# Three more of 28 key sums formed on GpSimd, and a newly computed order of all instructions

## The chip, the cores and the metric

One core of a Trainium2 chip runs the whole program. Its engines work side by side and meet at semaphores: PE (TensorE, matrix products), PEld (its weight loads), DVE (VectorE), ACT (ScalarE), POOL (GpSimd) and SP, which only issues DMAs. The metric is the device time of one execution in microseconds. The kernel before took 998.01 us (median of three runs, 996.77 to 999.7).

## The reference

For 8 batches, 8 heads, 576 positions and head size 64, the kernel computes linear attention with random features and feeds its output to a gated network:

```
phi(x)  = exp(x omega^T - |x|^2/2 - max) / sqrt(128)       x = q or k, scaled by 64^(-1/4)
num     = phi(q) (phi(k)^T v),   den = phi(q) sum_s phi(k) + 1e-6
x       = num / den, as rows of 512                        4608 tokens
out     = silu(x w_in) w_out                               512 -> 2048 -> 512
```

The sum over positions of phi(k), one vector of 128 features for each head, is what this document calls the key sum.

## The kernel before, in words

**Attention.** Heads are taken in pairs: 32 pairs n = 0 to 31, four to a batch. For a pair, PE projects keys and queries (`project` L554, and the shared middle block L560) into PSUM; DVE takes maxima (L569, L567) and shifts (L575); ACT (L592), for some pairs DVE (L600, L597) and then ACT, makes the exponentials `hk` and `hq`. PE forms phi(k)^T v (L713), and the key sum. DVE multiplies `hq` with the key sum and adds up (L701, `denom`), and takes the reciprocal `rd` (L706). POOL scales `hq` by it (L731), PE transposes it (L737) and forms the numerator (L773). Pairs 0 to 3 get their key sum as a column of another product (L651); the other 28 in one of two ways:

```
def zsum_direct(n, ps):          # pairs 4 to DIRECT - 1: PE alone, fp32
    for j in range(2):
        nc.tensor.matmul(..., sides_of[:, j], e[:, MID], ...)          # L641
        for i in range(4):
            nc.tensor.matmul(..., ones, e[:, 5 * j + i], ...)          # L643
def zsum(n, ps):                 # pairs DIRECT to 31: after POOL's five sums and a split
    for i in range(2):
        nc.tensor.matmul(ps[:, : 2 * M], ones_r, zp[:, i], ...)        # L635, fp32r
```

In the second way POOL first adds the blocks of `hk` into `t` (two of L615, one L617, two L621), rounds that to fp32r (`zp`, L626) and takes the rest (L630). PE then needs two fp32r products over 256 columns in place of ten fp32 products over 128.

**The network.** Every fp32 product of the network is made of three fp32r products (high by high, high by low, low by high). The first three batches go through both layers in the usual way: 16 steps f of 128 hidden units each, L948 for the first layer, L1194 for the second. The rest goes through a seven-product block scheme (L1033 first layer, L1147 second). The weights come in as 64-bit numbers: SP loads them, ACT and DVE rebuild fp32 words (L871, L873, L877 on DVE), POOL rounds to fp32r (L890) and takes the rest (L894). The 16 expansion weights w0 to w15 are needed by L948 at step f = 0 to 15 of the first batch, so all of this falls into the first 180 us, beside the attention of the early pairs.

**The order.** Nothing is scheduled on the chip: each engine runs its queue in the order in which the program was written. A planner in the kernel (`Plan.run`) makes that order before the build. It walks through all units of work with a table of costs (`COST` and `Plan.cost`), waits that it thinks worth taking (`WAIT_PE` and the like) and a key for each unit; the keys are moved by a long table of numbers (`SHIFTS`). The mark DIRECT also decides that for pairs after it the middle projection of the next pair shares a PSUM bank with a transpose (`mid_turn`), and that the small transpose of phi(k)^T v (L721) is issued inside a transpose unit; both issue the same matmuls.

Of the kernel before, what the change touches and what calls it, by code (L numbers as in the profile page):

```python
# [36 lines left out]
DIRECT = 8  # L37
# [18 lines left out]
for _f in range(16):  # L56
# [37 lines left out]
EASE = 0.075  # L94
# [11 lines left out]
    "nb": (0.29, 0.37), "vo": (0.3, 0.4), "dv": (1.25, 1.35), "tt": (0.54, 0.72), "ssum": (0.66, 0.745), "den": (3.41, 3.49),  # L106
# [10 lines left out]
    "AIBFNlBoBOAIAIAIAIApBkCNAIAIAIAIAIAIAIFBAIE3BkBpAIDrXvX-AIgAN4AIIrAIHRAISPAIA4AIAI-4AIAI+1m0E1AQY+BlAIAIV2GuVU"  # L117
    "SBLvMTDIWaBdE4g0N6BTSRSySyICKqsIR1gAAIEsNFA9fLBbECHyAIAIOAAIAUDL3PB5KVQqAmYoNLIWKmJSFLR6CSSkCNQnRQkVmxAIAIMQGa"
    "IfNyCEB5FigAQjAIsXAIowAI0OAIk7AIDxatOoF1gMqeAQCzXoVkB5AIAIFADkF5DzMcNKLNLLXVXXAIAIOwC2BmA3AIAIFvgANfFxj-AYSuAy"
    "McFlDlAIAIAIBAAIAIqUuwAIDsAIAIKxNGRn-4Q2r5S4MrmOiZ9nQbQSAIAINyCxBzAIPSDxCNenNIQVDD4DAIFPAQE2AI2BTGMtCy-4AIrhAI"  # L120
    "EcbS2qy0rA4lxxV7AIAIAIAIB9AIG3AIAwDECfMcs7Bgucbo-41sWs-4e793rN+ThC9aaOAfvmAIUH2y55sUlN740mPt-1h7821N-43g72-4l0"
    "E2o0zDr6kXx-YJ6s2X5WlO9I-4AIFDv7B2AI6Lu5I0UecHAIpivfe4bjX2TvOnTydYdOatC5E3LHLjxRMABFaSbJTaw289ejIQjbk+iselsruu"
    "tDyttvecpw-47QE2rZV4MadOm9Wwmfe8+t-WUGmK3abhpwFofCuzpdUDAIgIR4hCsbAiV3A6kV1tiDSjjzZavXGEBTH+AxCYKNAIAIis28YRmD"
    "EdkkOLdtqq4EAIAyA+p7lYAIHQDU0LgfrqAyYE1+9L-21oAIypYkcxoqYoZQ-WTKbdS+eg1Ci1Zd1q+wj5AIPai5RTGLbSsE1NJepCSpOA0jlx"
    "NB2GEiGdgCX3otpcn+otWkjcoVe5iXbUo1mhBf78wOVzlO7lrmqmmnfiBk3+avT+FCXRz3-j0MlfdiRab0iMN3i0baW6l7g4rd7iHfmhvjzkHD"
    "AJTjgZKdcGvcPLdHlYKefKdCT1nFM5k2RNblYanVw1GneWAIecUwt4fMhuZpR9Iwa5Ij69ZLfJvcAIEpF+BQQlAJjmCTRZcPCmNTHthxfUZ-AI"
    "BRXmYLQAIZR3ldNQq4S9FaOTCkOsMghgdKWyAIAIWAAIBcEUGeDOAIBSEZCMAIJhNWhaoGXG0lAIdJAIAIBjAIAIAIAIAIRpAIBQZtzlAgoFAI"
    "AIOoKSgpJONZHIAIprCgHvp7kijCrAjzn6AwAOAIBpAwPYnPCpLdMEqGXPAICPsvw4W09aOPLxRxBfIAAIKIARH+B8AIFHKfeUdnGXIvAIAIPg"
# [64 lines left out]
)  # L193
HOT = 100.0
PULSE = 0.24
IDLE = 1.237
PAD = 1.63
EARLY = 0.9

# [80 lines left out]
class Plan:  # L280
# [20 lines left out]
    def cost(self, u):  # L301
# [1507 lines left out]
```

## Time and profile before

| | |
|---|---|
| median of three runs | 998.01 us |
| the profiled execution | 997.93 us, of which 996.1 us span from the first instruction to the last |
| PE busy | 978.1 us (98%) |
| DVE / ACT / POOL busy | 744.2 / 634.7 / 380.6 us |
| granted TensorE clock | 0.995 of full speed on average |
| PE share of the chain that ended last | 80%, DVE 10% |

The span is what the trace covers; 1.8 us lie around it. Busy time is a union of instructions, so PE at 98% means that it had nothing in flight for 18 us. In a timeline a matmul's duration is its latency; how long it holds PE is read from one start to the next. An fp32 product shows as two records, an fp32r product as one.

### The profile page before, as it was taken

The numbers are of one execution on the slowest core, as the hardware profiler recorded it, in microseconds if no ns is written. First come the engines' busy times: TensorE is split into PE (matmuls) and PEld (weight loads), VectorE is DVE, ScalarE is ACT, GpSimd is POOL, SyncE is SP. The second block draws the span as 40 slices with busy tenths as digits, with TensorE's granted clock in tenths as the row PEclk, the third lists the DMA queues.
The fourth block names the chain that finished last, engine by engine and source line by source line (L and its number), as shares of the span: only waits on it lengthen the run. The fifth ranks groups of instructions, "written<-read, shape, count | busy, mean of one in ns | idle before, by whom it ended". The sixth has DMA issues, their size and how long they took to land.

```text
span 996.1 us, 17264 instructions
## 1 busy us (share of the span) xinstructions
PE 978.1 (98%) x5748; PEld 786.4 (79%) x5748; DVE 744.2 (75%) x1851; ACT 634.7 (64%) x1231; POOL 380.6 (38%) x483
## 2 busy tenths in 40 slices
PE   8999999999999999999999989999999999999998
PEld 7878877778787877777778778878888877888886
DVE  6999889676877557898676999895359977556853
ACT  6988677356666667867788666579676444334541
POOL 0255654777878786556672033223021000000000
PEclk8999999999999999999999999999999999999999
DMA  9787777687776877678887667866545787555582
GB/s 347 263 268 253 272 233 258 198 283 245 232 244 221 292 251 222 193 229 306 295 275 252 206 222 239 261 215 195 190 151 170 231 275 230 190 193 189 187 290 86
DMA packets 107592, 232.94 MB, mean 234 GB/s; under 512 B 14704, under 2 KB 39408, under 8 KB 107504
## 3 DMA queue, kind: packets, MB, share of 16 engines
q1 hardware_dynamic: 107344, 231.58, 70.6%
q8 instruction: 46, 0.75, 0.3%
q14 instruction: 42, 0.34, 0.1%
q10 hardware_dynamic: 160, 0.26, 0.1%
HBM read 182.52 MB, written 49.28 MB: 233 GB/s over the span
## 4 chain that ended last, share of the span: by engine, by line
PE 80%; DVE 10%; ACT 4%; POOL 3%; DMA 2%; issue 2%; SPq 0%; POOLq 0%; DVEq 0%; ACTq 0%
PE ps_acc L1033 19%; PE ps_acc L1147 15%; PE ps_acc L1194 11%; PE ps_h L948 7%; PE ps_fx L948 4%; PE ps_att L554 3%; PE ps_att L1147 3%; PE ps_att L1033 2%; PE ps_att L713 2%; PE ps_h L1147 2%; DVE prod L701 1%; PE ps_att L773 1%; PE ps_att L737 1%; PE ps_h L1033 1%; PE ps_fx L1147 1%
## 5 line engine op out<-in xcount | busy, mean ns | idle before, releaser
L1033 PE MATMUL ps_acc<-w,x 128*128 128x512 f32 x816 | 197.8, 396 | 0.0
L1033 PEld LDWEIGHTS ps_acc<-w,x 128*128 128x128 f32 x816 | 150.5, 188 | 33.9 <-DVE w L1080 0.3
L731 POOL TENSOR_TENSOR hq<-hq,rd 128x384 f32<-128x384 f32 x84 | 75.4, 922 | 167.1 <-DVE rd L706 166.9
L1194 PE MATMUL ps_acc<-wo,gh 128*128 128x512 f32 x384 | 123.1, 401 | 0.0
L1147 PE MATMUL ps_acc<-w,x 128*128 128x512 f32 x426 | 107.7, 395 | 0.2 <-DVE w L1137 0.2
L948 PE MATMUL ps_h<-x,w 128*128 128x512 f32 x384 | 102.7, 402 | 1.6 <-POOL w L894 0.6
L1147 PEld LDWEIGHTS ps_acc<-w,x 128*128 128x128 f32 x426 | 79.4, 188 | 18.8 <-DVE w L1137 0.9
L948 PEld LDWEIGHTS ps_h<-x,w 128*128 128x128 f32 x384 | 68.8, 188 | 18.2 <-POOL w L894 1.1
L1194 PEld LDWEIGHTS ps_acc<-wo,gh 128*128 128x128 f32 x384 | 68.6, 188 | 14.2
L1194 PE MATMUL ps_acc<-wo,gl 128*128 128x512 f32 x192 | 75.4, 393 | 0.0
L1147 PE MATMUL ps_acc<-gh,x 128*128 128x512 f32 x196 | 69.6, 396 | 0.0
L701 DVE CUSTOM_DVE_ANT_0 prod<-hq,ps_att 128x128 f32<-128x128 f32 (+1 forms) x170 | 48.8, 287 | 14.4 <-PE ps_att L635 8.6
L615 POOL TENSOR_TENSOR t<-hk 128x256 f32<-128x256 f32 x48 | 38.8, 823 | 47.3 <-ACT hk L606 30.1
L1091 DVE TENSOR_TENSOR gl<-gf,gh 128x512 fp32r<-128x512 f32 x48 | 42.5, 888 | 16.0 <-ACT gf L1087 16.0
L948 PE MATMUL ps_fx<-x,w 128*128 128x512 f32 x192 | 49.4, 398 | 0.0
L1147 PEld LDWEIGHTS ps_acc<-gh,x 128*128 128x128 f32 x196 | 36.8, 188 | 8.6
L537 ACT ACTIVATE nat<-nat 128x576 f32<-128x576 f32 x58 | 39.9, 695 | 4.8 <-DMA nat<-kn 3.4
L1194 PEld LDWEIGHTS ps_acc<-wo,gl 128*128 128x128 f32 x192 | 36.0, 188 | 8.4 <-DVE gl L1091 0.4
L948 PEld LDWEIGHTS ps_fx<-x,w 128*128 128x128 f32 x192 | 35.2, 188 | 7.8 <-issue 0.2
L747 ACT COPY en<-ps_att 128x384 f32<-128x384 f32 x56 | 27.0, 491 | 18.6 <-PE ps_att L737 13.2
L1147 PE MATMUL ps_acc<-gl,x 128*128 128x512 f32 x98 | 38.3, 391 | 0.0
L569 DVE TENSOR_REDUCE smq<-ps_att 128x4 f32<-128x512 f32 x44 | 29.0, 683 | 9.9 <-PE ps_att L554 9.4
(475 smaller groups left out, 2408.2 us busy)
## 6 DMA issues: line engine op xcount, KB each, us to landing
x<-ws SPq DMA_DIRECT2D x84, 512.0 KB, 3.6
x<-wt SPq DMA_DIRECT2D x44, 512.0 KB, 3.7
wo<-wo_d SPq DMA_DIRECT2D x32, 512.0 KB, 4.4
x<-wo_d SPq DMA_DIRECT2D x64, 256.0 KB, 3.2
rawq<-qT SPq DMA_DIRECT2D x30, 352.0 KB, 5.0
rawk<-kT SPq DMA_DIRECT2D x30, 352.0 KB, 4.3
v<-v SPq DMA_DIRECT2D x28, 320.0 KB, 4.0
nat<-kn SPq DMA_DIRECT2D x29, 288.0 KB, 4.3
```

The source lines that it names most:

```text
L537: nc.scalar.activation(nat, nat, AF.Square, scale=SCALE * 0.5**0.5)
L554: nc.tensor.matmul(ps[:, i * M : (i + 1) * M], raw[r, o : o + P], oms[r], start=True, stop=True)
L569: nc.vector.tensor_reduce(m[:, 5 * j : 5 * j + 4], ps.rearrange("p (c m) -> p c m", m=M), AX.X, ALU.max)
L615: nc.gpsimd.tensor_tensor(t[:, step], e[:, 5 * step : 5 * step + 2], e[:, 5 * step + 2 : 5 * step + 4], ALU.add)
L701: nc.vector.tensor_tensor_reduce(out=prod[r], in0=e[r, c], in1=z[r, j * M : (j + 1) * M], scale=1.0, scalar=GUARD, op0=ALU.mult, op1=ALU.a ...
L731: nc.gpsimd.tensor_tensor(e[:, c], e[:, c], rd[:, c].unsqueeze(2).broadcast_to([P, 3, M]), ALU.mult)
L747: nc.scalar.copy(T["en", n][:, 3 * g * P : 3 * (g + 1) * P], T.pop(("t", n, g)))
L948: nc.tensor.matmul(ph, w[:, i], x[:, j], start=k == 0 and n == 0, stop=k == NK - 1 and n == 2)
L1033: nc.tensor.matmul(ph, ws[:, u, kk * P : (kk + 1) * P], o[:, x], start=i in (0, 1, 4) and kk == 0 and n == 0, stop=kk == 1 and n == 2, ski ...
L1091: nc.vector.tensor_tensor(gl, T.pop(("gf", t, f)), T["gh", t, f].bitcast(F32), ALU.subtract)
L1147: nc.tensor.matmul(T["qb", p, chain][d], w[:, u, d * P : (d + 1) * P], x, start=i in (0, 1, 4) and s == 0 and n == 0, stop=s == NS - 1 and ...
L1194: nc.tensor.matmul(T["po", t][j], g[:, js], w, start=f == 0 and n == 0, stop=f == NF - 1 and n == 2)
```

## The change

DIRECT falls from 8 to 5, so that pairs 5, 6 and 7 (the sixth to the eighth) get their key sums through POOL and fp32r as pairs 8 to 31 did. Some costs of the planner and its waits are set anew, and the table of keys is a new one, so that the order of every engine changes.

```diff
-DIRECT = 8
+DIRECT = 5
-STAY = 9.083
+STAY = 20.466
-CALM = 0.133
-JOIN = 7.97
-WAIT_PE = 0.223
-WAIT_ACT = 0.222
-WAIT_DVE = 0.181
-WAIT_POOL = 0.175
-HASTE = 2.024
+CALM = 0.163
+JOIN = -0.122
+WAIT_PE = 0.281
+WAIT_ACT = 0.128
+WAIT_DVE = 0.175
+WAIT_POOL = 0.019
+HASTE = 8.0
-    "nb": ..., "vo": (0.3, 0.4), "dv": (1.25, 1.35), ...
+    "nb": ..., "vo": (0.555, 0.575), "dv": (1.375, 1.46), ...
 SHIFTS = (
-    "AIBFNlBoBOAIAIAIAIApBkCNAIAIAIAIAIAIAIFBAIE3BkBpAIDrXvX-AIgAN4AIIrAIHRAISPAIA4AIAI-4AIAI+1m0E1AQY+BlAIAIV2GuVU"
...
+    "AIAINlAIA4AIG7AIAIAIAKATGfAIALARAIAIHbGMFBAIE3BkBpAIDrFzI1IPgADuAIDoAIUiAIkqAIR1AIAI-4DCAIAIH1AIAIAIEVAIAIlvL3T7"
...
-IDLE = 1.237
-PAD = 1.63
+IDLE = 3.287
+PAD = 2.265
```

Over the whole program PE issues 24 fewer of L643, 6 fewer of L641 and 3 fewer of the filler products L506 (which stood in a wait near the start), and 6 more of L635. POOL issues 21 more instructions: 6 of L615, 3 of L617, 6 of L621, 3 of L626 and 3 of L630. DVE, ACT and SP have as many instructions of each kind as before. The PE queue changes between fp32 and fp32r products 248 times after its first L948, in place of 252.

**PE at the key sum of the sixth pair.** Before, it stands in the middle of the second layer's products of an early step (`sides` and `ones` are constants, `hk` the exponentials):

```order
L1194 MATMUL ps_acc<-wo,gl 128x512
L641 MATMUL ps_att<-hk,sides 128x128
L643 MATMUL ps_att<-hk,ones 128x128 x4
L641 MATMUL ps_att<-hk,sides 128x128
L643 MATMUL ps_att<-hk,ones 128x128 x4
L560 MATMUL ps_fx<-oms,rawk 128x128
L1194 MATMUL ps_acc<-wo,gh 128x512 x2
```

Now, in PE's queue (`zp` is what POOL made of `hk`, `w_1091` the expansion weight w3):

```order
L721 MATMUL ps_acc<-ident,kt 128x128
L560 MATMUL ps_acc<-oms,rawq 128x128
L635 MATMUL ps_fx<-zp,ones_r 128x256 x2
L554 MATMUL ps_att<-oms,rawk 128x128 x8
L948 MATMUL ps_fx<-x_415,w_1091 128x512 x3
```

The ten fp32 products became two fp32r products, and they stand earlier: before the first product with w3, where they stood behind w4's.

**POOL at the same place.** Before, its queue goes from the scaling of the fifth pair (L731) straight to the weights w3 (`w_1050`) and w4 (`w_1121`):

```order
L894 TENSOR_TENSOR wo<-w_812,wo 128x512
L731 TENSOR_TENSOR hq<-hq,rd 128x384 x3
L890 CAST w_1050<-w_1025 128x512
L894 TENSOR_TENSOR w_1050<-w_1025,w_1050 128x512
L890 CAST w_1121<-w_1090 128x512
L894 TENSOR_TENSOR w_1121<-w_1090,w_1121 128x512
```

Now the sixth pair's sums stand in between (w3 is `w_1091`, w4 `w_1117`):

```order
L731 TENSOR_TENSOR hq<-hq,rd 128x384 x3
L615 TENSOR_TENSOR t<-hk 128x256 x2
L617 TENSOR_TENSOR t<-t 128x2x128
L621 TENSOR_TENSOR t<-t,hk 64x128 x2
L890 CAST w_1091<-w_1055 128x512
L626 CAST zp<-t 128x256
L890 CAST w_1117<-w_1079 128x512
L894 TENSOR_TENSOR w_1117<-w_1079,w_1117 128x512
L630 TENSOR_TENSOR zp<-t,zp 128x256
L894 TENSOR_TENSOR w_1091<-w_1055,w_1091 128x512
```

All seven sums of the pair stand ahead of the rest of w3; its rounding went in between.

**DVE at the words of w13.** Before, the last of the three word instructions (L877 on `w_2030`) ends a short run, and the reduction of the eighth pair (L701) comes behind it:

```order
L546 TENSOR_REDUCE smq<-nat 128x9
L600 TENSOR_TENSOR hq<-ps_att,nbq 128x512
L600 TENSOR_TENSOR hq<-ps_fx,nbq 128x512
L1091 TENSOR_TENSOR gl<-gf,gh 128x512
L871 TENSOR_SCALAR w_2030<-wraw 128x512
L873 SCALAR_TENSOR_TENSOR w_2030<-wre,w_2030 128x512
L877 SCALAR_TENSOR_TENSOR w_2030<-wraw,w_2030 128x512
L701 ISA prod,den<-hq,ps_att 128x128
```

Now (the words of w13 are `w_2088`; the run begins with the end of the eighth pair's reduction):

```order
L706 RECIPROCAL rd<-den 128x9
L569 TENSOR_REDUCE smq<-ps_att 128x4
L575 TENSOR_REDUCE smq<-smq 128x2x4
L575 TENSOR_REDUCE nbq<-smq 128x2x4
L877 SCALAR_TENSOR_TENSOR w_1939<-wraw,w_1939 128x512
L871 TENSOR_SCALAR w_2033<-wraw 128x512
...
L1091 TENSOR_TENSOR gl<-gf,gh 128x512 x2
L871 TENSOR_SCALAR w_2088<-wraw 128x512
...
L873 SCALAR_TENSOR_TENSOR w_2088<-wre,w_2088 128x512
L597 TENSOR_SCALAR hk<-ps_att,nbk 128x128
L877 SCALAR_TENSOR_TENSOR w_2088<-wraw,w_2088 128x512
```

Ahead of w13's last word instruction DVE now has one whole reduction more (ten L701, ten reads, one L706), four more of L569, four more of L600, one more of L1091, six more of L575 and one more each of L567 and L597, and of no kind fewer. On PE, ahead of the first L948 with w13, there are 24 more of L554, nine more of L737 and one more of L560, and the three direct sums (30 products) are replaced by six of L635.

## Rows read from the trace of the kernel before

**Rows 1.** First part of the page: busy time, share, instructions.
```profile
PE 978.1 (98%) x5748; PEld 786.4 (79%) x5748; DVE 744.2 (75%) x1851; ACT 634.7 (64%) x1231; POOL 380.6 (38%) x483
```

**Rows 2.** Windows: stretch, length, busy of PE, PEld, DVE, ACT, POOL; clock; DMA.
```profile
8.00:14.00 6.00, 5.84 (x40) 5.35 (x40) 5.48 (x13) 3.09 (x9) 0.00 (x0) 0.50 1.04 415
...
0.00:60.00 60.00, 53.48 (x475) 48.19 (x476) 48.49 (x140) 47.74 (x145) 13.01 (x21) 0.94 0.83 297
60.00:171.00 111.00, 110.38 (x673) 88.28 (x673) 99.40 (x237) 82.96 (x156) 61.40 (x59) 1.00 0.76 261
```

**Rows 3.** Timeline of PE, direct sums of the sixth and eighth pair: start, duration.
```profile
87.74 0.38 PE L641 MATMUL ps_att<-hk,sides 128*128 128x128 f32 x2
...
89.97 0.39 PE L560 MATMUL ps_fx<-oms,rawk 128*128 128x128 f32 x2
...
150.49 0.48 PE L641 MATMUL ps_att<-hk,sides 128*128 128x128 f32 x2
...
152.74 0.71 PE L1194 MATMUL ps_acc<-wo,gh 128*128 128x512 f32 x2
```

**Rows 4.** Timeline of PE at the ninth pair's sum, the first in fp32r.
```profile
196.08 0.40 PE L635 MATMUL ps_att<-zp,ones_r 128*128 128x256 f32 x2
196.32 0.63 PE L1194 MATMUL ps_acc<-wo,gh 128*128 128x512 f32 x2
```

**Rows 5.** Groups of POOL by line, all 24 key sums: busy us, mean ns; idle before.
```profile
L615 POOL TENSOR_TENSOR t<-hk 128x256 f32<-128x256 f32 x48 | 38.8, 823 | 47.3 <-ACT hk L606 30.1 <-ACT hk L592 17.1
L621 POOL TENSOR_TENSOR t<-t,hk 64x128 f32<-64x128 f32 x48 | 24.2, 504 | 21.8 <-ACT hk L592 18.9
L617 POOL TENSOR_TENSOR t<-t 128x256 f32<-128x256 f32 x24 | 19.0, 790 | 1.8
L630 POOL TENSOR_TENSOR zp<-t,zp 128x256 fp32r<-128x256 f32 x24 | 18.8, 783 | 1.8
L626 POOL CAST zp<-t 128x256 fp32r<-128x256 f32 x24 | 11.5, 481 | 1.4
```

**Rows 6.** Timeline of POOL at the weight w13.
```profile
153.38 0.61 POOL L890 CAST w<-w 128x512 fp32r<-128x512 f32 x1 [4.45 <-DVE w L877]
154.07 1.30 POOL L894 TENSOR_TENSOR w<-w,w 128x512 fp32r<-128x512 f32 x1
```

**Rows 7.** Timeline of PE at the first products with w13 and inside w15's.
```profile
156.51 2.91 PE L948 MATMUL ps_fx<-x,w 128*128 128x512 f32 x12
...
172.79 2.56 PE L948 MATMUL ps_h<-x,w 128*128 128x512 f32 x10 [0.63 <-POOL w L894]
```

**Rows 8.** Timeline of DVE: shifts, a split and one whole reduction.
```profile
150.18 0.68 DVE L600 TENSOR_TENSOR hq<-ps_fx,nbq 128x512 f32<-128x512 f32 x1
150.78 0.68 DVE L1091 TENSOR_TENSOR gl<-gf,gh 128x512 fp32r<-128x512 f32 x1
...
153.23 0.28 DVE L701 CUSTOM_DVE_ANT_0 prod<-hq,ps_att 128x128 f32<-128x128 f32 x1
...
156.51 0.22 DVE L706 RECIPROCAL rd<-den 128x9 f32<-128x9 f32 x1
```

**Rows 9.** DVE's L873: group from 60 to 171 us; durations min/median/max, whole run.
```profile
L873 DVE SCALAR_TENSOR_TENSOR w<-wre,w 128x512 uint32<-128x512 uint32 x24 | 20.0, 835 | 1.0 <-ACT wre L857 0.3
...
L873 DVE SCALAR_TENSOR_TENSOR w<-wre,w x32: 675/692/1595, 23.5 to 176.0; 128x512 uint32<-128x512 uint32 x32
```

**Rows 10.** Timeline of PE: the longest idle times in the middle; one at L635.
```profile
354.26 0.38 PE L635 MATMUL ps_fx<-zp,ones_r 128*128 128x256 f32 x1 [0.42 <-POOL zp L626]
...
581.50 1.31 PE L713 MATMUL ps_fx<-hk,v 128*64 128x128 f32 x20 [1.52 <-ACT hq L592]
584.63 0.49 PE L554 MATMUL ps_h<-oms,rawk 64*128 64x128 f32 x2 [0.84 <-ACT hq L592]
```

**Rows 11.** Timeline of PE near the start: projections behind a wait, the filler products.
```profile
8.16 2.08 PE L554 MATMUL ps_acc<-oms,rawk 64*128 64x128 f32 x16 [2.02 <-DMA rawk<-kT]
...
10.75 1.49 PE L506 MATMUL ps_acc<-ones 128*128 128x128 f32 x6
```

More of the change, by code (lines that the diff above doesn't have):

```diff
@@ L93 @@
 COLD = 8.5
-EASE = 0.075
+EASE = 0.086
 FORMS = {"s1": 0, "s2": 0, "m": 0, "m2": 0, "proj": 2, "kv": 3, "num": 3, "kvnum": 3}
@@ new lines @@
+    "orwx2PkVrJAIMOWenkVZwSQS6A5GwpXg5Q6Fah7lhkDajs1bl7FnNzlmFhQcrbsgrceUsGfilwZacfEPDfGpHUqjUXAIoVPIo0AILWdEdgMFtE"
+    "r1GuDSaBWbgOcoNbJYf3KZBcK+pojewOLEQ+VmC9E31PAI9sAqAIZ0AIml838H-4gqU+QpueyZJ0AITARTKxAU3ESxvHF5FFQoxrXvVlKhECCi"
+    "AICUAILgFdJVARAIDZGOqhDKAuDKEgcpZF-g+7YXPLE1-jW1AIFVD6vTvHAIulggsB-4y6IDxJxyZJ4dAIle-QE1Jzjjexj1xpqBK8KzTJCZDl"
+    "E+CVwLBcF5VvExNfCJBSbnCiJ5JlG6IpKeBcRvDkJ8BcBcBcBBJWZFXwJCDBh9EjFjAKCAr6joBCYtKEJUHyATRWFcWG7u3DCwj8-4-4u05tXj"
+    "5m4j279Prnvs44RExe-1yEuufE0mA8hBz887irzb9OLHxLG0hSxanCxrwp0BQR3x1adluIOwWGumhN-Xu1FFk1Knp5n84kfhWWrHH7H9AjXtAI"
@@ new lines @@
+    "ApFBCucpEgEgEtLBVWIgHMCcAI38d7AgcySeLCLqBFEgSAfKWwNNk1TOT5hmJgUvJtFUpQEyOLBhAIBYDoAQBlUiUv22qeKkh-FboEAIBklYhI"
+    "AaBGAIAIAIC9DXxEgKXpjgNXCLQiHtlfPCTWANAIudBIHXdVV5DkagIvNSGjW5S7I+bADoZPAIAIGoV2CFFsNIxwZwlv4AXCY7ohHCfQhZj9NQ"
+    "NEAkEXGGOemqW9ntT+O7Bvo9dH-4UFF9KnDgGfA4Q2MFtRASLtHCM3eCByLwIYNlAdL2AIAIc1AIFtBRD+D0nrX7PzFnYkXdYoyReRU-GUAIAN"
+    "AIYDYKITnRvGWSAIAh4Ra03MezK5gFhBZVB+o0STVIcfexV5n5BTJ3C4JFQPQ9gaUwAIVvRYF9AIKHw9uKD0A-Z3LNGUHrLJFR-4EzGLDPDPNF"
+    "CCondFEUAzDPD9qB-cUmCADxQqHuHCCftFFBcKe-bxvyFMeHECdtAIHFEmCQEZ6EQ3upBtL5AIBLAIwRTgkI-4eMhpOJcy6kCJ5FAIAIlVTXrA"
@@ new lines @@
+    "gliahpAVDC+jtX7+GQezZNWq+7PrtXSUoFngozrwr+Ifl8xFL+b9AIlogsBtjXmOwjhh-K9e6psoj7H7UANbAIvBt4iaktTRIxXYAIQhxwa0ro"
+    "x9juAIpQfvz8Jyq1JWUQfqWUh8PNtpy8dVUHeGYMwY7a5zm2aIcDB30m3mshi1AId4bPe+a7iNOjR-fJgNhXbfpXGpFgD-2LFGK4pOhLL8OBA3"
+    "B7vMiO2EQ1vNAIcwOhzm7SMYCz8gls8Y3wBouegQ2yAIxUAI45A0g9JvBulgAIv3rxeTlu4XnVgaAIbyVqF2pNIUyOtk2XxveoTH5fMzG7AIJd"
+    "bF5UBGw-AvE90WS9re5d9W0D5K4l6J+pFVvLsOTBD6jklw4AFflGHTCfC64xQnERGEEtF-AIfYF7AIF8DhKQDrE7F7F4NRMCNBLsAIXEoMIbIV"
+    "EcLuMcXpJhEtSAMbFZGHFyGYsmKBEtDxAlGzHRAIOHA5AIPYAIAICZAIDSYviQyK5W20MDKl4FgBCvDTDygPozK-AI-ESy-4FrCxEMAbAcCaBM"
@@ new lines @@
+    "IuBxBRXRpaJRVBCFByB8jFATAbAIAqAICmLnJINaF9AI95GAAf3-AMFcw4ZrYsmABOGRJIHFJjzLDMPaBKBFM3JfMrstTXoQAIAIFEDcZfBHCG"
+    "AdFSTje2TvMlayMAaWWITwAiAIJMGTNVJDHWP4AIIJlDDtBMq44WVDi2DTRp55iIETE34W-hOpAI1aExXVd-ZDbR9LMbAIAU+v+v84HIHTjlJN"
+    "aovu+UVTxqBVAIDwu5+vDM+UiyJKtZ+MSCUfE22ADrAIg6bxsb6BC4xuAIMyPQ0-0i21rnNlZ0FTRI2XTtrVvbD7AIWSfTng-4SUGnSzHUQ5lR"
+    "ZWh0YdkdnlPFOaN+KMF1MIfylbOvjxGuFa82B7AItFCbEYyu+Jk6-46vFFD-kepOxPCvAIa-aV-izFw1jqzdAIAI-Dm+zVcDbJJ4d1Amtzs5pR"
+    "h3w9AIAI6Xpx3yu9o7AITGC2HPkVcqMiP7NA5rs-J4IPBfOOEykUIzMSJjq6juhiSdYkBqJTNCmwIQqEAIDMS6Z8GOYGGlAsCTBulscgrFcmQl"
@@ new lines @@
+    "F13Jf8bzJ+SoJUs6SisaTsLFU1UgAIGGQPhkBYCHhauxVIAIHV-b-4nxRDCIckO1BrTDVoTYeVAIB1uO44dPHMCIuEtrAIqVCDAITiAIAIAIAr"
+    "AIPZCW-23QPlQNXANly0QZBDBqSyENJzsivc+bzcpaDK5czPnxDRAIcRHEZuUg118247CWAPdJwej7DXJsJBGXET7p0qoUfhIHtggecwZO3MCE"
+    "T4FdJtNWBWjnwNGhe7KPEUGa-teiKjDQEFOZILiQnNbuCAmuILF+JfAIElZDQDAITJRdep74VvYraQx1FMHjev7lTnS+XMb9ZCQrFXvMPVJ4sX"
+    "GiAOK+bo3FFvAIFvPmvKu47ThCwZH5C6-e4i0uv59t7nTstq+TAI2hPdtXCOcsttmk0owLjTlIok+3nGz8+pjl59tiiFQKWoIunj4OVUwdVUlk"
+    "uCIaAIEqlmHL1ACCK5j6lBWxrBvA65t9bND2XsakxpNPPCK4Ggs+Bnr6siadQjjrwnVxCf7shEciX6904FxelcVviwGsXUMMCkD7QeCkVvOyCk"
@@ L193 @@
+    "oPs2mDeNprl1l2rImepGmlrRnOi-h0pdrkoMlD"
 )
@@ L319, in cost @@
         if n[0] in ("kv", "num") and n[1] < SHARE:
-            return 2.25, 2.42
+            return (2.26, 2.47) if kind == "kv" else (2.18, 2.35)
         if kind == "kw" and n[1] < SHARE:
-            return 0.24, 0.35
+            return 0.15, 0.28
         if kind == "wd" and n[-1] == 0:
```

127 lines of the change are left out of this document (51 added, 76 removed).

## The prediction

> **What bounds the kernel now.** The page's first part comes first: PE has work in flight for 978.1 of 996.1 us, DVE for 744.2 and POOL for 380.6 [rows 1]. So PE is the bound, and there are only 18 us of idle PE time to win or to add to; whatever shortens PE's own work shortens the run, as long as PE does not wait instead. The windows come second, since a mean of 98% can hide a stretch with another limit. From 60 to 171 us PE has 110.4 of 111.0 us, but DVE has 99.4 too, and POOL 61.4 [rows 2]. In this stretch two engines are nearly full at once: DVE idles for 11.6 us there, and for 11.5 us before 60 us. Third, the timeline at the hand-over between them. The weight w13 is ready at 154.07 + 1.30 = 155.37 us and PE begins with it at 156.51, a margin of 1.1 us; for w15 the margin is gone, and PE waits 0.63 us for POOL, which has its words from DVE [rows 6, 7]. POOL itself had waited 4.45 us for DVE before w13 [rows 6], so DVE is what makes weights late. All three key sums that change lie in or just before this stretch.
>
> **What PE loses.** The direct sum of the sixth pair holds PE from 87.74 to 89.97, 2.23 us, that of the eighth from 150.49 to 152.74, 2.25 us [rows 3]; the seventh issues the same ten products, so I take 2.24 for it too: 6.72 us. The fp32r form holds PE from 196.08 to 196.32, 0.24 us [rows 4]; three of them cost 0.72. Net: -6.0 us, all of it on the engine that sets the end. The four changes fewer between fp32 and fp32r I set at nothing: at the eighth pair the direct sum stood alone between fp32r products and was only 0.02 longer for it. The merged middle blocks and transposes issue the same matmuls: 0.
>
> **What POOL gains.** One key sum on POOL is (38.8 + 24.2 + 19.0 + 18.8 + 11.5) / 24 = 4.7 us [rows 5], three are 14.0. POOL idles for 49.6 us between 60 and 171 [rows 2], so its own time is covered. If that cover were gone, PE would wait at L635; where POOL was late before, it cost 0.42 us behind one of its last two steps [rows 10]. Between nothing and two such waits at each of three sums, 2.5 us, I take 0, because the sixth pair's sum stands in PE's queue behind all products with w0, w1 and w2. The weights behind the sums in POOL's queue, w3 and w4, come up to 4.7 us later; the first must end before PE's L948 with w3, which now comes 1 us of PE work (eight L554) behind that sum, so POOL's last step for w3 has about that to end in. I take 0 there too.
>
> **What DVE gets, and when.** DVE's instructions are the same in kind and number, but ahead of w13's last word instruction there are now more. One reduction takes from 153.23 to behind 156.51, 3.4 us; an L600 takes 0.60 from start to start (150.18 to 150.78) [rows 8]. Four L600 are 2.4; four L569 and one L1091, which read a tile of the same size, I estimate at the same 0.60, so 3.0; eight small ones at L706's 0.22 are 1.8. Together 10.6 us more work in front of the words of w13. PE, on its side, comes to w13 a little earlier: 24 L554 more (eight take 2.08 us at half clock [rows 2, 11], so 3.1 at full), nine transposes and a middle block at half and whole of an fp32 product's 0.22, 1.2, against 6.0 less for the sums: -1.7 us. Adding the 1.1 us of margin, the words of w13 may come 0.6 us earlier than before at most, with 10.6 us more to do: 11.2 us of DVE's idle time must be filled, out of 11.5 before 60 us and nearly as much from there to 153 us. Each microsecond that is not filled is a microsecond that PE waits, since its queue is in order: behind L948 with w13 stand all of the next step's products, and ACT's silu and DVE's splits wait for them.
>
> How much is filled no row shows; the bounds are 0 and 11.2 us of PE wait. Below 0 only the 0.63 us at w15 can go. I take 1.1 us, a tenth of the upper end: DVE's idle moments here are waits for PE and ACT in the attention of single pairs, and what was moved ahead is the same kind of work of another pair, that is, something to do in just those moments; and the nearest row for a late weight is the 0.63 us at w15 [rows 7], two of which are 1.3.
>
> POOL's 14 us also cost DVE something. L873 takes 675 ns at the least and 835 ns on average from 60 to 171 us [rows 9]: 24 times 0.16 is 3.8 us lost to something beside it, while POOL was busy for 61.4. By that rate 14 us more of POOL add 0.9 us to L873, which is inside the bounds above. The Trainium skill speaks against this change more strongly here: SBUF — State Buffer, "Who interferes with whom", says that a DVE instruction with two SBUF inputs and a GpSimd instruction that reads SBUF contend for a lock, and that the later one blocks until the other is through. L873 has two SBUF inputs, and its longest, 1595 ns [rows 9], agrees with a full block. If each of the 18 reading additions and differences and the three roundings blocked one DVE instruction for its whole length, DVE would lose all 14 us instead of 0.9, and by that, an estimate, PE would wait 13 us more and the sum would be 1006.
>
> **The start.** Keys are now loaded and projected first, then queries. The wait of 2.02 us at 8.16 and the half clock from 8 to 14 us, which costs 3 us, stand there now [rows 2, 11]. The second projection can follow the first one transfer later, but in SP's queue the next pair's keys stand two transfers behind the ones for which PE waited, so I expect one such pause in another place. The three filler products, 1.49 us, stood in front of products that waited [rows 11]: 0. Bounds: 3 us better with no pause at half clock, 3 us worse with two; I take 0.
>
> **The middle and the end.** Between 578 and 585 us PE waited 1.52 and 0.84 us for ACT, which waited for a crowded DVE [rows 10]. A new order has such places elsewhere; I keep them at the same sum, with bounds of 2.4 us better and 2.4 worse. The end of the run is not touched.
>
> **The sum.** The profiled execution took 997.93 us, 1.83 around its span of 996.1, and stands within 0.1 us of the median of 998.01. 997.93 - 6.0 + 1.1 = 993.0 us.
>
> **Rivals.**
> *The weights hold PE (the other side).* Place: L948 with w13 to w15, near 155 to 173 us. DVE fills none of its idle time with the work moved ahead; PE waits 11.2 us. For it: DVE is at 90% and the margin at w15 is already negative. Against it: DVE's queue would have to stay as patchy as before with more work at hand. 997.93 - 6.0 + 11.2 = 1003.1. It makes the run slower from a wait of 9.1 us on. (By the skill's rule above it would come out here too.)
> *The gain is given back there.* Half of it is filled, PE waits 5.6 us: 997.5. The same margins speak for it, and that the new queue is as tight at w14. Against it: nothing but that POOL and DVE waited for each other rather than being full.
> *The new order is better elsewhere too.* The waits at 581 and 584 us go (2.4) and the one at w15 (0.6), and nothing comes instead: 997.93 - 6.0 - 3.0 = 988.9. For it: they belong to one crowded place, with PE otherwise at 99%. Against it: 18 us of idle is little, and the rest is start and end.
>
> **How the numbers follow.** The forecast, with PE waits between 0 and 3 us more than before, gets 0.50 (its own range 991 to 995); the gain given back 0.21; slower 0.12; better elsewhere 0.17. 0.3% of 998, 3 us, is about what a measurement of this kernel can tell from no change, so faster means below 995 and slower above 1001. Faster: the forecast but for its upper edge, 0.48, and 0.17, so 0.65. Same: 0.21 and 0.02, so 0.23. Slower: 0.12. The range goes from 986 (the better rival and 3 us at the start) to 1001: what lies above is most of the slower rival, 0.1, and what lies below under 0.1.
>
> **What would show it.** Right: PE busy near 972 us or a little under; six L635 more with 0.24 us from start to next; POOL busy near 394; PE idle between 150 and 200 us not over 3 us. Wrong: PE's releaser at L948 is POOL's L894 for several microseconds with DVE's L877 behind it; L873's mean well over 835 ns from 60 to 171 us; a second stretch of half clock; or PE idle of over 24 us in all.

## The result and the profile after

The changed kernel takes 1008.42 us (median of four runs, 1005.03 to 1009.20) against 997.88 beside it: 1.0095 times as long, 95% interval 1.0082 to 1.0108. It is slower by 10 us where 5 us less were forecast. Its profiled execution took 1005.03 us with a span of 1003.2; it is the fastest of the four, so its rows show 7.1 of the 10 us.

The page's first part after, beside [rows 1]:

```profile
PE 977.0 (97%) x5688; PEld 781.3 (78%) x5688; DVE 749.8 (75%) x1851; ACT 627.1 (63%) x1229; POOL 397.3 (40%) x504
```

PE has 60 records fewer (33 fp32 products less, at two records each, and six fp32r products more), but its busy time fell by 1.1 us only, and its idle time rose from 18.0 to 26.2: -1.1 + 8.2 = +7.1, the whole difference of the spans. The three new key sums on PE are nearly as short as forecast (0.24 each); from L635 to the next start it takes 0.41, 0.23 and 0.29 us:

```profile
71.13 0.48 PE L635 MATMUL ps_fx<-zp,ones_r 128*128 128x256 f32 x2
71.54 0.48 PE L554 MATMUL ps_att<-oms,rawk 64*128 64x128 f32 x2
...
97.51 0.40 PE L635 MATMUL ps_att<-zp,ones_r 128*128 128x256 f32 x2
97.74 0.39 PE L560 MATMUL ps_att<-oms,rawq 128*128 128x128 f32 x2
...
150.04 0.45 PE L635 MATMUL ps_fx<-zp,ones_r 128*128 128x256 f32 x2
150.33 0.62 PE L1194 MATMUL ps_acc<-wo,gh 128*128 128x512 f32 x2
```

The windows of [rows 2], after:

```profile
8.00:14.00 6.00, 5.02 (x47) 4.35 (x45) 5.79 (x16) 5.48 (x18) 0.00 (x0) 1.00 1.04 409
0.00:60.00 60.00, 55.24 (x500) 49.20 (x500) 51.42 (x156) 47.72 (x147) 16.00 (x25) 1.00 0.81 287
60.00:171.00 111.00, 102.29 (x595) 80.21 (x597) 101.02 (x224) 77.15 (x148) 68.88 (x73) 0.95 0.73 248
```

The start is better: the half clock of 8 to 14 us is gone (1.00 for 0.50), and PE idles for 4.8 us before 60 us where it idled for 6.5. The loss is in the third row: PE has 102.3 us of 111 where it had 110.4, and the granted clock is 0.95. The timeline of PE after shows in single rows where it waits (start, duration, in brackets the wait ahead and who ended it):

```profile
60.99 0.52 PE L737 MATMUL ps_fx<-ident,hq 128*128 128x128 f32 x3 [1.12 <-ACT en L747]
...
72.97 1.16 PE L554 MATMUL ps_att<-oms,rawk 64*128 64x128 f32 x14 [0.94 <-ACT hq L592]
76.37 0.94 PE L948 MATMUL ps_fx<-x,w 128*128 128x512 f32 x3 [2.24 <-DVE den L701]
...
125.08 0.37 PE L554 MATMUL ps_fx<-oms,rawk 64*128 64x128 f32 x1 [1.14 <-ACT hq L592]
129.58 1.62 PE L948 MATMUL ps_h<-x,w 128*128 128x512 f32 x3 [2.60 <-ACT gf L1087]
```

At 76 us PE stands with the first products of w3 before bank fx, which holds the sixth pair's key sum until VectorE's reduction has read it; at 129.6 before bank h, which ScalarE's SiLU has not read. Behind both of these waits the clock falls (not behind those at 61 and 73 us, of 1.12 and 0.94). The windows at the second:

```profile
125.00:130.00 5.00, 2.32 (x20) 2.00 (x21) 3.81 (x9) 4.66 (x11) 3.12 (x5) 0.90 0.94 320
130.00:135.00 5.00, 5.00 (x27) 3.05 (x28) 4.93 (x12) 2.62 (x4) 1.28 (x2) 0.50 0.18 50
135.00:140.00 5.00, 5.00 (x35) 3.97 (x33) 4.62 (x5) 1.54 (x4) 4.15 (x5) 0.92 0.83 274
```

0.50 is 1.2 GHz. By their clocks these three slices cost 3.4 us, 75 to 85 us (0.78 and 0.88) another 1.7. At w13 to w15, where the forecast had put the danger, there is nothing: PE idles for 0.88 us from 150 to 200 us, for 1.03 before. The chain of waits of before runs over PE's own instructions without a break from 65 to 164 us; of the 140 us from 60 to 200, its pieces on PE add up to 124, those on VectorE to 12. After, it leaves PE at 48.8 us and comes back at 129.6; of the same 140 us PE has 56, VectorE 43, ScalarE 18 and weights on their way 15. A piece of it (start, us, what):

```profile
64.53 5.15 DMA wraw<-w_out
...
69.78 0.68 ACT wre L857
...
70.48 1.28 ACT L592
71.78 0.36 ACT hq L592
...
72.98 0.29 DVE prod L701
```

A weight on its way, ScalarE's exponent of it, a table load, the exponentials, VectorE's reduction: here TensorE is not on the path. VectorE shows the same from its side. Between the ninth and the tenth of its last word instructions (L877) now stand the whole reduction of the sixth pair, and behind it maxima and splits, and 12.4 us pass:

```profile
69.22 1.30 DVE L877 SCALAR_TENSOR_TENSOR w<-wraw,w 128x512 uint32<-128x512 uint32 x1
...
72.18 0.29 DVE L701 CUSTOM_DVE_ANT_0 prod<-hq,ps_fx 128x128 f32<-128x128 f32 x1
...
81.64 0.69 DVE L877 SCALAR_TENSOR_TENSOR w<-wraw,w 128x512 uint32<-128x512 uint32 x1
```

Before, it was 5.2 us from the ninth to the tenth:

```profile
71.97 0.68 DVE L877 SCALAR_TENSOR_TENSOR w<-wraw,w 128x512 uint32<-128x512 uint32 x1
...
77.13 0.68 DVE L877 SCALAR_TENSOR_TENSOR w<-wraw,w 128x512 uint32<-128x512 uint32 x1
```

The last of the 32 L877 starts at 183.8 us, 6.9 later than the 176.9 of before, which is nearly the whole 7.1 (count, ns min/median/max, first and last start):

```profile
L877 DVE SCALAR_TENSOR_TENSOR w<-wraw,w x32: 675/691/1774, 24.1 to 183.8; 128x512 uint32<-128x512 uint32 x32
```

### The profile page after: what moved, and what is told of

It reads as the page before. It is cut to its first block, busy times and chain, and to the rows that moved or that the text cites. A ratio compares the mean times of both kernels' runs of the same rounds, so it can differ in the third digit from the quotient of the medians.

```text
span 1003.2 us, 17152 instructions
## 1 busy us (share of the span) xinstructions
PE 977.0 (97%) x5688; PEld 781.3 (78%) x5688; DVE 749.8 (75%) x1851; ACT 627.1 (63%) x1229; POOL 397.3 (40%) x504
## 4 chain that ended last, share of the span: by engine, by line
PE 82%; DVE 10%; ACT 3%; DMA 2%; issue 2%; SPq 0%; DVEq 0%; ACTq 0%
PE ps_acc L1033 18%; PE ps_acc L1147 16%; PE ps_acc L1194 11%; PE ps_h L948 7%; PE ps_att L554 4%; PE ps_fx L948 4%; PE ps_att L1147 3%; PE ps_att L1033 2%; PE ps_att L713 2%; PE ps_h L1147 2%; PE ps_att L773 2%; DMA wraw<-w_out 1%; PE ps_att L737 1%; DVE prod L701 1%; PE ps_h L1033 1%
## 5 line engine op out<-in xcount | busy, mean ns | idle before, releaser
L731 POOL TENSOR_TENSOR hq<-hq,rd 128x384 f32<-128x384 f32 x84 | 76.9, 941 | 172.5 <-DVE rd L706 122.3
L948 PE MATMUL ps_h<-x,w 128*128 128x512 f32 x372 | 99.1, 403 | 3.7 <-ACT gf L1087 3.5
L948 PEld LDWEIGHTS ps_h<-x,w 128*128 128x128 f32 x372 | 67.7, 189 | 20.2 <-POOL zp L626 2.8
L615 POOL TENSOR_TENSOR t<-hk 128x256 f32<-128x256 f32 x54 | 42.9, 812 | 50.7 <-ACT hk L606 34.2
L1091 DVE TENSOR_TENSOR gl<-gf,gh 128x512 fp32r<-128x512 f32 x48 | 41.2, 862 | 29.0 <-ACT gf L1087 28.9
L948 PE MATMUL ps_fx<-x,w 128*128 128x512 f32 x204 | 53.7, 402 | 2.2 <-DVE den L701 2.2
L948 PEld LDWEIGHTS ps_fx<-x,w 128*128 128x128 f32 x204 | 37.7, 190 | 11.4 <-issue 2.4
L621 POOL TENSOR_TENSOR t<-t,hk 64x128 f32<-64x128 f32 x54 | 28.5, 529 | 45.5 <-ACT hk L592 42.4
L701 DVE CUSTOM_DVE_ANT_0 prod<-hq,ps_att 128x128 f32<-128x128 f32 (+1 forms) x130 | 37.2, 286 | 9.7 <-PE ps_att L635 5.3
```

What stands on the lines that cost most here:

```text
L615: nc.gpsimd.tensor_tensor(t[:, step], e[:, 5 * step : 5 * step + 2], e[:, 5 * step + 2 : 5 * step + 4], ALU.add)
L621: nc.gpsimd.tensor_tensor(es[r, j], es[r, j], e[r, MID], ALU.add)
L701: nc.vector.tensor_tensor_reduce(out=prod[r], in0=e[r, c], in1=z[r, j * M : (j + 1) * M], scale=1.0, scalar=GUARD, op0=ALU.mult, op1=ALU.a ...
L731: nc.gpsimd.tensor_tensor(e[:, c], e[:, c], rd[:, c].unsqueeze(2).broadcast_to([P, 3, M]), ALU.mult)
L948: nc.tensor.matmul(ph, w[:, i], x[:, j], start=k == 0 and n == 0, stop=k == NK - 1 and n == 2)
L1091: nc.vector.tensor_tensor(gl, T.pop(("gf", t, f)), T["gh", t, f].bitcast(F32), ALU.subtract)
```

## The experiments

To part the sums from the order, the order of either kernel was kept as it is, instruction by instruction, and single instructions in it were exchanged, left out or moved. Some of these kernels leave out work that the result needs; they are there for their time alone. Times are medians, and ratios are to runs of the kernel before beside them, with 95% intervals.

**1. The old order with the new sums.**
```diff
+ at = max(i for i, u in enumerate(seq) if u["name"][:3] == ("exp", n, "k")) + 1     # n = 5, 6, 7
+ seq[at:at] = sums(n, 0..4), sums_high(n), sums_low(n)
- zsum_direct(n, ps)
+ zsum(n, ps)
```


> The kernel before, its order kept instruction by instruction; only the key sums of the sixth to eighth pair change: GpSimd's seven instructions stand right behind the pair's last key exponential, and the two fp32r passes stand where the ten fp32 matmuls stood, in the same bank. Theory A (the sums are worth what was computed, the new order lost it): three sums save 3 x (2.24 - 0.24) = 6.0 us, no new wait of TensorE over 1 us, clock at full speed from 15 us on: about 992 us. Rival B (the sums on GpSimd cost the time themselves, by later weights or by VectorE): no gain, 998 us or more, up to the 1008 of the kernel after, with TensorE waiting for weights or for the pair's reduction at 60 to 175 us.

1006.38 us (1.0083, 1.0070 to 1.0096): theory A fell at once. PE's timeline and POOL's name a part of it:

```profile
102.89 0.90 PE L737 MATMUL ps_att<-ident,hq 128*128 128x128 f32 x3 [1.31 <-POOL hq L731]
```
```profile
95.82 1.89 POOL L615 TENSOR_TENSOR t<-hk 128x256 f32<-128x256 f32 x2
...
101.82 2.24 POOL L731 TENSOR_TENSOR hq<-hq,rd 128x384 f32<-128x384 f32 x2
```

The seventh pair's block of sums stands between two pieces of the sixth pair's normalization, and PE waits for the second. So the place in POOL's queue had to be taken out of the question.

**2. The sums in POOL's idle gaps; the sums alone; PE's saving alone.**
```diff
+ ("norm", 4, 2): [(5, 0), (5, 1)], ("wlo", "in", 3): [(5, 2), (5, 3), (5, 4), (5, "high"), (5, "low")], ...   # gaps; unused: the same
- for i in range(4):
+ for i in range(4 if n == 4 else 0):                                                                       # cut
```


> As the first experiment (the order before, key sums of pairs six to eight on GpSimd, two fp32r passes in the old place), but the 21 GpSimd instructions stand in the idle gaps that GpSimd's queue shows before (63.5, 67.8, 84.7, 92.5, 96.7, 101.5, 133.5, 136.7, 143.0 us) and not in one block behind the exponential. Theory P (what cost 10 us there was the block's place: it held up weights at 69 us and the normalization at 97 us): the 6.0 us come through, 992 us, at most 995 with VectorE's slower weight words. Rival D (between 60 and 180 us VectorE, 95% busy, ends as late as TensorE, and GpSimd's sums slow its weight words by 4 to 5 us): no gain, 997 us or more.

> The kernel before with the same 21 GpSimd instructions in the same gaps added, their result unused: TensorE still forms the key sums in ten fp32 matmuls. It prices GpSimd's sums alone. Theory P: nothing waits, 998 to 999 us. Rival D: VectorE's weight words grow by 4 to 5 us over the 135 us and TensorE waits for what VectorE forms: 1001 to 1004 us.

> The kernel before, with the direct key sums of pairs six to eight cut to the two matmuls of the middle chunk (eight of ten left out, so the denominators of three pairs lack most of their terms); nothing on GpSimd. It prices TensorE's saved time alone: 24 matmuls of 0.22 us, 5.3 us. Theory P: 992.5 us. Rival D: TensorE runs into its partners' results, TensorE's idle time at 60 to 180 us grows by what was taken out, 996 us or more.

The sums in the gaps take 1001.59 us (1.0033, 1.0021 to 1.0045), the sums added but unused 1001.15 (1.0023, 1.0012 to 1.0033). PE's time cut by 5.3 us, with nothing added, takes 999.65 (1.0013, 1.0002 to 1.0024). (VectorE is busy for 107.5 of the 120 us from 60 to 180, 90% and not the 95% of the expectation.) The last of the three is the key of the case: five microseconds of PE's work taken out of the stretch gain nothing. VectorE's last weight instruction, L877, tells it (count, ns min/median/max, first and last start); before, and with the cut:

```profile
L877 DVE SCALAR_TENSOR_TENSOR w<-wraw,w x32: 678/685/1653, 24.3 to 176.9; 128x512 uint32<-128x512 uint32 x32
```
```profile
L877 DVE SCALAR_TENSOR_TENSOR w<-wraw,w x32: 676/685/1656, 24.6 to 176.4; 128x512 uint32<-128x512 uint32 x32
```

Of 5.3 us saved by then, 0.5 arrive. (The median is even 1.4 us up, but this trace, 0.5 ahead at 176 us, ends 3.5 behind, at 999.6 against 996.1, with nothing changed between: PE waits 0.96 us at 671 and 1.23 at 830 us, as it does in the trace of the memsets of experiment 3 and not before. What came on top is in this run not the cut's doing; whether the 1.4 us is stays open.) In their place PE waits, with the cut, in three new places:

```profile
93.77 1.16 PE L554 MATMUL ps_att<-oms,rawq 64*128 64x128 f32 x14 [0.90 <-DVE den L701]
...
109.59 0.33 PE L721 MATMUL ps_fx<-ident,kt 128*128 128x128 f32 x1 [0.52 <-ACT xr L802]
...
159.19 0.52 PE L737 MATMUL ps_att<-ident,hq 128*128 128x128 f32 x3 [1.32 <-DVE hq L597]
```

These 2.7 us are what rows show; the rest lies inside busy time that the windows don't part. The chain has moved as after the change: of the 140 us from 60 to 200, 77 are on PE now (124 before), 42 on VectorE (12) and 11 on weights on their way.

**3. How the sums cost: memsets in their places.**
```diff
+ nc.gpsimd.memset(t, 0.0)      # or zp, for each of the 21 instructions; nothing is read
```


> The seventh experiment (21 GpSimd instructions more in GpSimd's gaps, result unused, 1001.15 us, VectorE's weight words 6.7 us longer) with each of the 21 replaced by a memset of 128x512, some 0.6 us each, which reads nothing: 12.6 us of GpSimd's time in the same queue places. If the sums cost by holding up GpSimd's own queue: 1000 to 1001 us as well, with VectorE's words as long as before. If they cost by what they do to VectorE's words while they read and write beside them: 998 to 999 us, words as long as before (56.5 us for 80 at 55 to 190 us); or, if any GpSimd access does it, longer words and 1000 us or more.

997.70 us (1.0000, 0.9989 to 1.0011): 12.1 us more in POOL's queue cost nothing by themselves. VectorE's three word instructions from 55 to 190 us (busy us, mean ns), before:

```profile
L873 DVE SCALAR_TENSOR_TENSOR w<-wre,w 128x512 uint32<-128x512 uint32 x27 | 22.2, 824 | 1.0 <-ACT wre L857 0.3
L877 DVE SCALAR_TENSOR_TENSOR w<-wraw,w 128x512 uint32<-128x512 uint32 x27 | 19.8, 743 | 0.4
...
L871 DVE TENSOR_SCALAR w<-wraw 128x512 uint32<-128x512 uint32 x26 | 14.5, 567 | 0.6 <-DMA plain<-w 0.6
```

with the sums added and unused:

```profile
L873 DVE SCALAR_TENSOR_TENSOR w<-wre,w 128x512 uint32<-128x512 uint32 x27 | 24.6, 912 | 0.9
L877 DVE SCALAR_TENSOR_TENSOR w<-wraw,w 128x512 uint32<-128x512 uint32 x27 | 22.0, 824 | 0.4
L871 DVE TENSOR_SCALAR w<-wraw 128x512 uint32<-128x512 uint32 x26 | 16.6, 647 | 2.4 <-DMA plain<-w 1.2 <-POOL w L894 1.2
```

and with memsets (line numbers are 11 higher):

```profile
L884 DVE SCALAR_TENSOR_TENSOR w<-wre,w 128x512 uint32<-128x512 uint32 x27 | 22.5, 832 | 0.9
L888 DVE SCALAR_TENSOR_TENSOR w<-wraw,w 128x512 uint32<-128x512 uint32 x27 | 19.8, 744 | 0.4
L882 DVE TENSOR_SCALAR w<-wraw 128x512 uint32<-128x512 uint32 x26 | 16.7, 652 | 0.6 <-DMA plain<-w 0.6
```

The two instructions with two SBUF inputs take 42.0 us before, 46.6 beside the sums, 42.3 beside memsets. The Trainium skill (SBUF — State Buffer, "Who interferes with whom") says just this: such a VectorE instruction contends with a GpSimd instruction that reads SBUF, not with one that only writes it. The third, with one SBUF input, is as long beside memsets (16.7) as beside the sums (16.6), without a loss of time. Memsets also wait for no exponential, and they are 12.1 us where the sums are 16.5, so that a part of the 2.9 us may lie in POOL's queue after all: beside the sums VectorE's L871 waits 1.2 us for POOL's L894, which it doesn't beside memsets.

**4. VectorE relieved.**
```diff
- nc.vector.tensor_scalar(bits, low, 29, None, ALU.logical_shift_right)
+ return
```
The first of three word instructions is left out (the second then takes `wre` in place of its result), in four kernels: before, before with PE's cut, the old order with the sums in the gaps, and after.

> The kernel before without the first of VectorE's three word instructions of each weight block (the low bits of the weights are left out, the second instruction ORs a finite word in their place): 32 instructions less, 26 of them between 55 and 190 us, 14.5 us of VectorE's time there. TensorE's work is unchanged. Theory D (VectorE and TensorE end that stretch together): TensorE then has it alone, and only its 2 us of waits at 60 to 200 us can go: 996 to 997 us. Rival O (VectorE is not the pace, what TensorE met in the eighth experiment were single waits of the order): 998 us, no change.

> The eighth experiment (direct key sums of pairs six to eight cut to two matmuls, 5.3 us of TensorE's time, which alone gained nothing) with the first word instruction left out as well. Theory D: with VectorE relieved TensorE's 5.3 us come through in full: 991 to 992 us, five less than without the cut. Rival O: they are lost in the order's waits again: 996 us or more.

> The sixth experiment (old order, key sums on GpSimd in its idle gaps, two fp32r passes, 1001.6 us) with the first word instruction left out. Theory D: VectorE has 14.5 us less and loses 7 to 8 us beside GpSimd's sums, so TensorE's saving shows: 991 to 994 us. Rival O: 998 us or more.

> The kernel after with the first word instruction left out. Theory D alone (the new order loses because VectorE is late): the waits at 60 to 185 us go with their half clock, 995 us or less. Theory A (the new order has waits of its own, behind the single banks and ScalarE's table changes, whatever VectorE does): the waits at 76 us and 129 us stay at 1.5 us or more each, and the time stays above 1003 us.

In this order they take 997.55 us (0.9994, 0.9985 to 1.0002), 996.65 (0.9986, 0.9974 to 0.9997), 997.80 (0.9998, 0.9987 to 1.0008) and 1004.43 (1.0067, 1.0050 to 1.0084). VectorE is part of it: relieved, the sums cost 0.25 us in place of 3.4, and the cut gains 0.9 us where it lost 1.4. By the end of the stretch the cut is 2.3 us ahead, without it and with it:

```profile
L877 DVE SCALAR_TENSOR_TENSOR w<-wraw,w x32: 676/688/1780, 24.3 to 176.3; 128x512 uint32<-128x512 uint32 x32
```
```profile
L877 DVE SCALAR_TENSOR_TENSOR w<-wraw,w x32: 678/691/1779, 23.8 to 174.0; 128x512 uint32<-128x512 uint32 x32
```

It is not all: of 5.3 us 0.9 arrive by medians and 2.3 by these rows, not the five of theory D. And the new order keeps its loss, with its waits in place:

```profile
62.50 0.88 PE L737 MATMUL ps_fx<-ident,hq 128*128 128x128 f32 x3 [2.62 <-ACT en L747]
...
78.11 0.93 PE L948 MATMUL ps_fx<-x,w 128*128 128x512 f32 x3 [2.42 <-DVE den L701]
...
130.20 1.34 PE L948 MATMUL ps_h<-x,w 128*128 128x512 f32 x3 [2.18 <-ACT gf L1087]
```

A third engine was relieved too, ScalarE, on top of the second of these four:
```diff
+ if 7 <= n <= 11: return      # in square(n, who)
```


> The eleventh experiment (direct sums cut by 5.3 us on TensorE, first word instruction of VectorE left out: 996.65 us, of the 5.3 us some 2.4 arrive by 200 us) with ScalarE's squares of pairs eight to twelve left out too, ten instructions of 0.68 us. Theory T (three engines end the stretch together, and TensorE's saving arrives as each partner is relieved): another 1 to 2.5 us, 994 to 995.5 us. Rival O (what is left are fixed places of the order, such as one bank and one table change): 996.5 us, no change.

996.92 (0.9989, 0.9980 to 0.9998): no change. ScalarE's total is not what holds back the rest.

**5. The new order without the sums.**
```diff
- sums, sums_high, sums_low of pairs 5 to 7 (e2: 5 and 6)
- zsum(n, ps)
+ zsum_direct(n, ps)      # e2
+ zsum_ones(n, ps)        # e9: four fp32r matmuls of ones
```


> The kernel after, its order kept; the sixth and seventh pair's key sums are again the ten fp32 matmuls, at the place and in the bank of the two fp32r passes, and GpSimd's fourteen instructions for them are left out. Theory A: 2 x 2.0 = 4.0 us more of TensorE, and the waits of the new order stay (about 2 us for bank fx behind the sixth pair's reduction, about 2.6 us for bank h behind the SiLU at 129 us): about 1012 us. Rival B: without the sums on GpSimd the waits go, with the half clock behind them: 4.0 - 4.8 to 4.0 - 10, about 1002 to 1008 us.

> The kernel after without GpSimd's 21 instructions for the sums of pairs six to eight; in their place TensorE adds four fp32r matmuls of 128 columns of ones (so these denominators are wrong), in place and bank of the two passes. It prices the sums in the new order. Theory A (the order's own waits): 1006 to 1008 us, the waits for banks fx and h at 76 and 129 us still there. Rival B: below 1002 us.

1009.51 (1.0108, 1.0094 to 1.0123) and 1007.45 (1.0098, 1.0083 to 1.0113). With none of the three sums on POOL (the second of the two) the new order is slow just the same; its wait for fx stands at 80 us with 2.57, its wait for h at 133 us with 2.18. In the first, 4 us more of PE's work make the new order 1.1 us longer only.

**6. The new order's waits taken out by moving work.**
```diff
+ ("z", 5): u["pools"] = ["acc"]                            # e3, e14, e16
+ move([("gl", 0, 7)], ("ssum", 10, "k"))                   # e4, e14, e16
+ move([("s2", 0, 7, j) for j in range(4)], ("s1", 0, 9, 0))
+ ("turn", 4, 2): u["pools"] = ["acc"]; move([("gl", 0, 0)], ("den", 5))      # e14, e16
```


> The kernel after; only the bank of the sixth pair's key sum is another (a free accumulator bank in place of fx). Theory A: the next first-stage group no longer waits for the pair's reduction to read fx: the wait of 2.24 us at 76.4 us goes, and with it the stretch of 0.78 and 0.88 clock at 75 to 85 us, worth some 1.7 us: about 1004.5 us. Rival: the second stage, which stands behind and needs all accumulator banks and the g whose low half VectorE forms after the reduction, waits in its place: 1008 us.

> The kernel after; the second-stage group of the eighth weight block (12 matmuls, 2.7 us, planned at 135 to 139 us) stands ahead of the first-stage group that waits 2.60 us for bank h, and the low half of its g is formed earlier on VectorE. Theory A: the wait is filled with work, and the half clock of 125 to 140 us (0.90, 0.50, 0.92: 3.4 us lost) does not come: 2.6 + 3.4 = 6.0 us less, about 1002.4 us. Rival C: the clock falls all the same or the time is only moved to the next wait: between 1005.8 (wait filled, clock not) and 1008.4 us.

> The kernel after with its order's four waits taken out by moving work, not by leaving any out: the third transpose group of the fifth pair and the sixth pair's key sum stand in accumulator banks in place of fx, the low half of the first g is formed ahead of the sixth pair's reduction, and the eighth weight block's second stage stands ahead of the first-stage group that waits for bank h. Theory A (beyond what GpSimd's sums cost, the new order loses by these waits and the half clock behind them, 6 to 7 us): it comes to where the old order with the sums stands, 1000 to 1003 us. Rival W (the waits only show that ScalarE and VectorE are behind, and come again at the next place): 1005 to 1008 us.

> The fourteenth kernel with VectorE's first word instruction left out as well. Theory A with D: both causes are gone and what is left is TensorE's saving, 995 to 998 us. Rival W: 1002 us or more, as with VectorE's relief alone (1004.4 us).

The first three take 1009.01, 1006.70 and 1007.17 us (1.0112, 1.0085 and 1.0095, each within 0.0025), the last, with VectorE relieved, 1003.09 (1.0057, 1.0045 to 1.0069). Rival W holds. In the fourteenth kernel (e14) the waits at 76 and 129 us are gone, that at 61 us is 1.64 us at 62 now, and PE stands here:

```profile
83.28 0.49 PE L560 MATMUL ps_att<-oms,rawk 128*128 128x128 f32 x2 [2.13 <-ACT hk L592]
...
143.42 1.27 PE L948 MATMUL ps_fx<-x,w 128*128 128x512 f32 x3 [2.61 <-DVE hk L600]
```

A wait taken out is met again at the next place where PE needs ScalarE or VectorE, and VectorE's last L877 starts at 184.2 us, as late as after the change. The waits were more a sign than the cause.

**7. The same cut of PE elsewhere.**
```diff
+ if n == 2 and t == 1 and 5 <= f < 11: continue      # in stage2
```


> The counterpart of the eighth experiment at another place: the kernel before with 24 matmuls of the second stage left out between about 250 and 310 us (the third product of six weight blocks of the second token block, so a correction term of the sum is missing there): 24 x 0.23 = 5.5 us of TensorE's time, in a stretch where VectorE is busy for 70%. Theory D (a microsecond of TensorE is worth what its stretch lets through): nearly all arrives, 992.5 to 993.5 us. Rival (the tight order gives back any saving of TensorE): 996 us or more.

998.03 us (0.9996, 0.9987 to 1.0006): the rival holds, and theory D's rule, that a microsecond is worth "what its stretch lets through", is too narrow. From 250 to 300 us PE idles for 1.6 us (0.15 before), and from 350 to 450 for 3.4 (1.1 before); there PE waits for the key sums on POOL (the profiled run, of 1001.23 us, is the slowest of its eleven, so these rows may show more than the median has):

```profile
353.29 0.39 PE L635 MATMUL ps_fx<-zp,ones_r 128*128 128x256 f32 x1 [0.90 <-POOL zp L626]
354.10 0.39 PE L635 MATMUL ps_fx<-zp,ones_r 128*128 128x256 f32 x1 [0.42 <-POOL zp L630]
...
375.44 0.38 PE L635 MATMUL ps_fx<-zp,ones_r 128*128 128x256 f32 x1 [1.42 <-POOL zp L630]
```

So also at 70% of VectorE this saving on PE did not arrive while the rest of the order stayed.

## Why the prediction was wrong

**The step that failed** first is "Net: -6.0 us, all of it on the engine that sets the end". The size is nearly right (three sums hold PE for 0.93 us in place of 6.72, so -5.8), its place on the path is not. PE busy for 110.4 of 111 us was read as PE alone setting the end. PE did set it (124 of 140 us of the chain), but a second path, over VectorE and the weights' loads, was hardly shorter; the chain goes over to it when PE has 5.3 us less. In the old order the saving alone brings VectorE's last weight 0.5 us forward and the median +1.4 us, not -5.3 (experiment 2). VectorE, 99.4 in the same row, is a part of that path and not the whole (experiment 4). The prediction had seen that two engines were "nearly full at once" and still priced PE's saving as if PE were alone.

**VectorE beside POOL** was set at 0.9 us, from L873 alone and from an average. Measured with the unused sums: POOL busy for 17.0 us more, VectorE's words 6.7 us longer (63.2 for 56.5), and 2.9 us of the kernel's time. The rule of a full block that was weighed there gave 14 us of VectorE; the runs lie between, 0.4 us for each of POOL's. The sign that was named for it did not show: after the change L873 has a mean of 828 ns from 60 to 171 us, under the 835 of before.

**POOL's own cover** held: no L635 waited over 0.2 us from 60 to 160 us.

**The new order** is the second and larger step that failed, "I take 1.1 us": it was priced by one wait at one place, w13 to w15. That place held. The loss came from elsewhere: PE's idle time changed by -1.8 us up to 60 us, +7.9 from 60 to 200, +2.1 from 450 to 650. The middle is inside its bounds; the start gained more than the 3 us allowed (1.8 of idle and the half clock), and it did not help: from 61 us on PE waits. The half clock behind a wait, 5.1 us, was priced at the start only, though "a second stretch of half clock" was named as a sign. It and PE's idle time of over 24 us are the two signs of being wrong that came true.

Put together, by medians and along this path: the sums in the old order, at the best places found, 998.2 to 1001.6, +3.4; the new order on top of it, 1001.6 to 1008.4, +6.8. Along the other path the parts are not the same: the new order without the sums is at 1007.45 us, and the sums on top of it add 1.0, which the intervals don't tell from nothing. By either path the order is the larger part. Its loss stays without the sums, with VectorE relieved (1004.4 against 997.8, 6.6) and for the most part with the four waits moved (1007.2 against 1001.6, 5.6; with VectorE relieved too, 1003.1 against 997.8, 5.3). The cause inside the order isn't settled. The rows show that VectorE's words fall behind by 6.9 us, with attention work ahead of them at 72 to 81 us, and that the chain runs over the weights' loads; no run put the words back in front. SP's issues of the weights wait for VectorE's L877, since three buffers are shared, but not longer than before (38.0 us from 50 to 200 us, 38.2 before), and a fourth buffer wasn't tried. No version that does the whole work was measurably faster than the kernel before.

## What to carry to other kernels

Where two engines are both near 90% or above in a stretch, don't count on a microsecond taken off one of them until an experiment says so; the cheapest one leaves the work out and looks at the time. In this order, written out in advance, two savings of over 5 us on the fullest engine did not arrive, one of them where VectorE was at 70%, so price a rewritten order by the slack of each hand-over, not by the sum of work. And look at what work moved to GpSimd costs VectorE: here 16.5 us of sums, which read SBUF, made VectorE's weight words 6.7 us longer, 4.6 of them in the instructions with two SBUF inputs.

## What the runs showed of the hardware

After TensorE had waited for 1.14 and 2.60 us within 6 us, it ran at 1.2 GHz from 130 to 135 us: these waits cost nearly as much again by the clock (3.4 us). Behind waits of 2.1 and 2.6 us in the fourteenth kernel it fell too (0.66 at 85 to 90 us, 0.88 and 0.78 at 140 to 150). A wait alone does not tell it: one of 1.5 us at 580 us left the clock at 1.00 from 580 to 585 us in the trace of before, and the same wait stands beside 0.66 in that of PE's cut. Memsets on GpSimd, 12.1 us of them, made VectorE's two-input word instructions 0.3 us longer; 16.5 us of sums that read SBUF made them 4.6 longer.
